# One visit of the array per attention chunk, reads on four quadrants, and two chunks scaled by GpSimd

## The chip, the cores and the metric

One core of a Trainium2 chip runs the whole program. The metric is the device time of one execution in microseconds (us), lower is better. A core has a matmul engine (TensorE, PE in the profile, its weight loads shown apart as PEld), three elementwise engines (VectorE = DVE, ScalarE = ACT, GpSimd = POOL) and a queue that issues transfers (SyncE = SP). Each engine works through its own list of instructions in order; semaphores tie the lists together.

## The reference

```python
# attention: batch 4, 8 heads, 576 positions, head_dim 64
scores = scale * np.matmul(q, k.transpose(0, 1, 3, 2))
gamma = 1.0 - 2.0 ** (-5.0 - np.arange(H))
Dmat = np.where(rel >= 0, gamma[:, None, None] ** rel, 0.0)   # rel = pos_i - pos_j
attn_out = np.matmul(scores * Dmat, v)
x = attn_out.transpose(0, 2, 1, 3).reshape(2304, 512)
# first feed-forward layer, 512 -> 2048 -> 512
h = x @ w_in;  x = np.maximum(0.01 * h, h) @ w_out
# second feed-forward layer, 512 -> 2048 -> 512
h = x @ w_in2; out = (h * np.cos(h)) @ w_out2
```

There is no softmax, so a head's attention can be carried as a running state: what earlier positions give to a query is the query times a 64x64 sum of key-value products.

## The kernel before

**Attention.** The 2304 tokens are cut into 18 chunks of 128, each of two sub-chunks of 64. A chunk's q, k and v for all 8 heads come in one 1 MB transfer (`load_chunk`, into two buffers by turns from chunk 4 on). VectorE scales q (`scale_q`, L219), and ScalarE (chunks 1, 2 and 4 to 7), GpSimd (3) or VectorE (the others) scales v (`scale_v`, L226, L231). Then:

- `scores` (L250): keys times queries, 16 matmuls of 64x64 on all four 64x64 quadrants of the array.
- `masks` (L266): VectorE multiplies the scores by the causal mask into SBUF.
- `values` (L281 and L295): masked scores times v (16 matmuls, L281), and keys times v, which is what the chunk adds to the state (16 matmuls, L295; 8 in a chunk that ends a sequence).
- `states` (L313, L315): VectorE adds that to the running state of each sub-chunk.
- `reads` (L328): state times queries, added to the values in PSUM, 16 matmuls (8 where a sub-chunk begins a sequence). A matmul reads the partitions of one head of a pair and writes the same partitions: only the two quadrants on the diagonal are used.
- `take` (L354): ScalarE scales the result out of PSUM into `xr`.

In the trace every one of these fp32 matmuls has two records, so 16 matmuls read x32.

**First layer.** Tokens go in five blocks (512, 512, 512, 384, 384). For each of 16 slices f of the hidden width there is a group H(j,f) of 12 matmuls (`h_mm`, L451), ScalarE's leaky ReLU out of PSUM (`leaky`, L476 or L741), its split into a high and a low part (L481/L745 on ScalarE, L486/L748 on VectorE), and two steps later a group O(j,f) of 12 matmuls (`o_mm`, L465). In steady state TensorE does H, O, H, O. `h_mm` alternates between two PSUM banks: `hp = psum[:, BANK_H + f % 2, :n]`. PSUM has eight banks: 0 to 3 hold O's sums, 4 and 5 are H's, 6 and 7 are the attention's.

**Order of the work.** Chunks 0 to 3 are done before block 0. Block 0 is written out by hand (the loop over `s` at the end): at step s TensorE does H(0,s), then, where `chunk_at` has a chunk, `values`, the next chunk's `scores` if due, O(0,s-2), `reads`. Meanwhile the weights of this layer are converted from 64-bit words on the fly: per slice VectorE does L397, L399, L403, L410 and, a step later, L422 (the low part), ScalarE L391, L392 and L419. H(0,f) needs L422 of its slice f. Chunks 4 to 7 are used in block 0 and loaded two chunks ahead: after `reads(i)` come `load_chunk(i + 2)` and, for chunks 8 and 9, `scale_q` and `scale_v` on VectorE in the middle of that conversion.

Blocks 1 to 4 and the second layer are ordered by a planner (`Plan`), which is fed tasks with rough durations and due times and plays them; each engine's order comes from it. The second layer is a Strassen-like scheme of `i_mm` (L1062) and an output product (L1191). Its weights are converted during blocks 1 to 4 (L949, L951, L935 to L946).

Of the kernel before, what the change touches and what calls it, by code (L numbers as in the profile page):

```python
# [19 lines left out]
P = 128  # L20
# [35 lines left out]
BANK_O, BANK_H, BANK_A = 0, 4, 6  # L56
# [91 lines left out]
def retention_ffn_ffn(  # L148
# [67 lines left out]
    def scale_q(i):  # L216
        q = ch_t[i][:, 0]

        nc.vector.tensor_tensor(out=q, in0=q, in1=itab_sb, op=ALU.mult)  # L219

    def scale_v(i):
# [8 lines left out]
        eng = nc.gpsimd if 0 < i < n_first else nc.vector  # L230
# [6 lines left out]
    def banks_of(i):  # L237

        return (6, 4, 0, 2)[i] if i < n_first else BANK_A

    def scores(i):
        b, ch = banks_of(i), ch_t[i]
        for p in range(NP):
            for x in range(2):
                for e, r in enumerate(halves):
                    t = slice(p * P + x * C, p * P + (x + 1) * C)
                    nc.tensor.matmul(  # L250
                        psum[halves[x], b + e, p * C : (p + 1) * C],
                        ch[r, 1, t],
                        ch[r, 0, t],
                        start=True,
                        stop=True,
                    )

    def masks(i):
        b = banks_of(i)
# [3 lines left out]
        else:  # L263
            pt = ap.tile([P, 2, NP, C], F32, tag="p", name="p_sb", bufs=1)
        p_t[i] = pt
        nc.vector.tensor_tensor(  # L266
            out=pt,
            in0=psum[:, b : b + 2, : NP * C].rearrange("p e (n c) -> p e n c", n=NP),
            in1=mask_sb.unsqueeze(1).unsqueeze(1).to_broadcast([P, 2, NP, C]),
            op=ALU.mult,  # L270
        )

    def values(i):
        b, ch, pt = banks_of(i), ch_t[i], p_t.pop(i)
        local = [(2 * i + x) % SUBS for x in range(2)]
        for p in range(NP):
            for x, tok in enumerate(halves):
                for e, r in enumerate(halves):
                    h = slice((2 * p + e) * D, (2 * p + e + 1) * D)
                    o = NP * C + p * C  # L280
                    nc.tensor.matmul(  # L281
                        psum[r, b + x, o : o + C],
# [3 lines left out]
                        stop=local[x] == 0,  # L286
                        skip_group_check=True,
                    )
        for p in range(NP):
            for x, tok in enumerate(halves):  # L290
                if local[x] == SUBS - 1:
                    continue
                for e, r in enumerate(halves):
                    h = slice((2 * p + e) * D, (2 * p + e + 1) * D)
                    nc.tensor.matmul(  # L295
                        psum[r, b + x, p * D : (p + 1) * D],
                        ch[tok, 2, h],
                        ch[tok, 3, h],
                        start=False,
                        stop=True,  # L300
                        skip_group_check=True,
                    )

    def states(i):
        b = banks_of(i)
        local = [(2 * i + x) % SUBS for x in range(2)]
        for x in range(2):
            if local[x] == SUBS - 1:
                continue
            new = ap.tile([P, NP * D], F32, tag="st", name="st", bufs=3)  # L310
            add = psum[:, b + x, : NP * D]
            if local[x] == 0:
                summed[i] = nc.vector.tensor_copy(new, add)  # L313
            else:
                summed[i] = nc.vector.tensor_tensor(out=new, in0=add, in1=state[2 * i + x], op=ALU.add)  # L315
            state[2 * i + x + 1] = new

    def reads(i):
        b, ch = banks_of(i), ch_t[i]
        local = [(2 * i + x) % SUBS for x in range(2)]  # L320
        for x in (1, 0):
            if local[x] == 0:
                continue
# [1112 lines left out]
```

## Time and profile before

| | |
|---|---|
| median of 3 runs | 876.35 us (874.76 to 878.08) |
| the profiled execution | 877.37 us, its span 875.6 us |
| PE busy | 847.6 us, 97% of the span |
| DVE busy | 601.1 us, 69% |
| ACT busy | 518.7 us, 59% |
| POOL busy | 1.7 us, 5 instructions |
| DMA | 193.3 MB, 62.7% of 16 engines' time |
| chain that ended last | PE 84%, DMA 7%, DVE 6% |

The span divides into a start (to about 64 us) in which VectorE's conversion sets the pace, blocks 0 to 4 of the first layer (to 495 us), and the second layer. "PEclk" is the clock that TensorE was granted, 1.00 being 2.4 GHz and 0.50 being 1.2 GHz. A row of the timeline is: start, length (us), engine, line, operation, output<-inputs, shapes, count, and in brackets the idle time of the engine before it with what ended it. The lengths of consecutive matmuls overlap slightly, so distances are best taken from start to start.

### The profile page before, as it was taken

Reading aid. Unit: us, or ns where it says so; the run is one execution under the profiler, and the core shown is the slowest. Engines: PE = TensorE matmul, PEld = TensorE weight load, DVE = VectorE, ACT = ScalarE, POOL = GpSimd, SP = SyncE. Lnnn points to the kernel's source line nnn. Section 1 sums busy time; section 2 is a strip of 40 time slices with the busy share of each in tenths; the row PEclk is TensorE's granted clock in tenths of the full one; section 3 lists DMA queues with packets and bytes.
Section 4 is the critical chain, followed back from the end, with each engine's and each line's share of the span. In section 5 each row is a group of like instructions: output and inputs, shape, how many; then the busy total and the mean of one; then the engine's idle time right before and its main releaser. Section 6 shows DMA issues by size and latency. Waiting matters only on the chain.

```text
span 875.6 us, 16272 instructions
## 1 busy us (share of the span) xinstructions
PE 847.6 (97%) x6288; PEld 779.3 (89%) x6288; DVE 601.1 (69%) x1187; ACT 518.7 (59%) x1112; POOL 1.7 (0%) x5
## 2 busy tenths in 40 slices
PE   6699979999999999999999999999999999999998
PEld 6577767778887888899999989999999999999998
DVE  5799684767776676676631278888897876765772
ACT  4787753545455545555632388777678765777650
POOL 0000000000000000000000000000000000000000
PEclk8899989999999999999999999999999999999999
DMA  9925402557657666665476398979988798474311
GB/s 360 417 78 208 158 1 86 173 177 230 188 215 232 182 230 192 230 207 191 147 293 270 88 315 283 335 249 409 310 288 264 260 369 334 158 268 181 132 49 73
DMA packets 91949, 193.30 MB, mean 221 GB/s; under 512 B 7648, under 2 KB 55264, under 8 KB 81632
## 3 DMA queue, kind: packets, MB, share of 16 engines
q1 hardware_dynamic: 91728, 191.92, 62.7%
q8 instruction: 49, 0.80, 0.4%
q10 hardware_dynamic: 144, 0.35, 0.1%
q14 instruction: 28, 0.23, 0.1%
HBM read 143.22 MB, written 49.02 MB: 220 GB/s over the span
## 4 chain that ended last, share of the span: by engine, by line
PE 84%; DMA 7%; DVE 6%; issue 1%; ACT 1%; SPq 0%; DVEq 0%; ACTq 0%
PE psum L1191 22%; PE psum L465 19%; PE psum L451 19%; PE psum L1062 19%; DMA ch<-in_qkv 4%; PE psum L328 2%; PE psum L250 1%; PE psum L281 1%; DMA mraw<-in_w 1%; PE psum L295 1%; DMA xq<-m 1%; DVE w L422 1%; DVE t L410 1%; DVE t L403 1%; DMA ws<-ws 1%
## 5 line engine op out<-in xcount | busy, mean ns | idle before, releaser
L451 PE MATMUL psum<-x_sb,w 128*128 128x512 f32 (+1 forms) x960 | 218.4, 377 | 10.6 <-DVE w L422 7.2
L1191 PE MATMUL psum<-g,wo 128*128 128x384 f32 x1152 | 222.3, 334 | 0.0
L465 PE MATMUL psum<-g,w 128*128 128x512 f32 (+1 forms) x960 | 214.4, 373 | 0.0
L451 PEld LDWEIGHTS psum<-x_sb,w 128*128 128x128 f32 x960 | 177.3, 191 | 37.5 <-DVE w L422 8.3
L1191 PEld LDWEIGHTS psum<-g,wo 128*128 128x128 f32 x1152 | 201.7, 188 | 0.0
L465 PEld LDWEIGHTS psum<-g,w 128*128 128x128 f32 x960 | 173.8, 188 | 24.4 <-DVE graw L704 0.4
L1062 PE MATMUL psum<-x,ws 128*128 128x384 f32 x576 | 114.5, 335 | 1.8 <-ACT psum L1164 1.3
L1062 PEld LDWEIGHTS psum<-x,ws 128*128 128x128 f32 x576 | 100.9, 188 | 2.8 <-ACT psum L1164 1.9
L748 DVE TENSOR_TENSOR g<-graw,g 128x512 fp32r<-128x512 f32 (+1 forms) x64 | 39.9, 624 | 68.4 <-ACT g L745 67.7
L1062 PE MATMUL psum<-x,wa 128*128 128x384 f32 x432 | 86.1, 334 | 0.0
L1062 PEld LDWEIGHTS psum<-x,wa 128*128 128x128 f32 x432 | 75.9, 188 | 0.0
L745 ACT CAST g<-graw 128x512 fp32r<-128x512 f32 (+1 forms) x64 | 36.2, 566 | 63.0 <-PE psum L465 62.5
L1118 DVE SCALAR_TENSOR_TENSOR h<-r,h 128x384 f32<-128x384 f32 x96 | 52.9, 553 | 24.5 <-ACT r L1115 24.2
L741 ACT ACTIVATE graw<-psum 128x512 f32<-128x512 f32 (+1 forms) x64 | 34.8, 543 | 51.4 <-PE psum L451 49.3
L1114 ACT ACTIVATE r<-r 128x384 f32<-128x384 f32 x96 | 50.4, 525 | 21.4 <-DVE r L1107 20.9
L1102 DVE SCALAR_TENSOR_TENSOR r<-n,h 128x384 f32<-128x384 int32 x96 | 52.9, 551 | 11.9 <-ACT n L1099 11.6
L1128 DVE TENSOR_TENSOR g<-h,g 128x384 fp32r<-128x384 f32 x96 | 52.6, 552 | 11.1 <-ACT g L1125 10.4
L1099 ACT ACTIVATE n<-h 128x384 int32<-128x384 f32 x96 | 49.3, 518 | 8.4 <-DVE h L1091 8.0
L1107 DVE SCALAR_TENSOR_TENSOR r<-n,r 128x384 f32<-128x384 int32 x96 | 53.1, 553 | 1.6
L1125 ACT CAST g<-h 128x384 fp32r<-128x384 f32 x96 | 48.6, 509 | 7.2 <-DVE h L1118 6.9
L1115 ACT ACTIVATE r<-r 128x384 f32<-128x384 f32 x96 | 50.5, 526 | 2.0
L1210 DVE SCALAR_TENSOR_TENSOR acc<-psum,acc 128x384 f32<-128x384 f32 x48 | 26.7, 556 | 16.4 <-PE psum L1191 15.3
(80 smaller groups left out, 795.8 us busy)
## 6 DMA issues: line engine op xcount, KB each, us to landing
ws<-ws SPq DMA_DIRECT2D x24, 1024.0 KB, 7.0
wo<-wo SPq DMA_DIRECT2D x24, 1024.0 KB, 6.5
wa<-wa SPq DMA_DIRECT2D x24, 768.0 KB, 6.4
ch<-in_qkv SPq DMA_DIRECT2D x17, 1024.0 KB, 7.4
mraw<-in_w SPq DMA_DIRECT2D x64, 256.0 KB, 3.4
x<-xq SPq DMA_DIRECT2D x21, 768.0 KB, 9.6
raw<-in_w SPq DMA_DIRECT2D x15, 1024.0 KB, 10.4
xq<-m SPq DMA_DIRECT2D x84, 128.0 KB, 5.0
```

Source lines behind the costliest of these rows:

```text
L451: nc.tensor.matmul(hp, wt[:, i, cols], x_t[lj, k][:, j, :n], start=(k == 0 and a == 0), stop=(k == KK - 1 and a == 2),)
L465: nc.tensor.matmul(psum[:, BANK_O + m, :n], wt[:, i, cols], gt[:, j, :n], start=(f == 0 and a == 0), stop=(f == NF - 1 and a == 2),)
L1062: nc.tensor.matmul(bank[BANKS[m]], a[:, hl, i, j * P : (j + 1) * P], x[:, j, v, :], start=m in (1, 5) and j == 0 and n == 0, stop=j == 1 a ...
L1099: t = add("ACT", 515, lambda: nc.scalar.activation(n_ap(), hb.ap, AF.Copy, scale=INV_2PI), [t], due, 0, nb.old)
L1102: nc.vector.scalar_tensor_tensor(out=r_ap(), in0=n_ap(), scalar=-C1, in1=hb.ap, op0=ALU.mult, op1=ALU.add)
L1107: nc.vector.scalar_tensor_tensor(out=r_ap(), in0=n_ap(), scalar=-C2, in1=r_ap(), op0=ALU.mult, op1=ALU.add)
L1114: t = add("ACT", 515, lambda: nc.scalar.activation(r_ap(), r_ap(), AF.Sin, scale=0.5), [t], due)
L1115: t = add("ACT", 515, lambda: nc.scalar.activation(r_ap(), r_ap(), AF.Square), [t], due)
L1118: nc.vector.scalar_tensor_tensor(out=hb.ap, in0=r_ap(), scalar=0.5, in1=hb.ap, op0=ALU.subtract, op1=ALU.mult)
L1125: t = add("ACT", 515, lambda: nc.scalar.copy(gb.ap[:, 0], hb.ap), [t], due, 0, gb.old)
L1128: nc.vector.tensor_tensor(out=gb.ap[:, 1], in0=hb.ap, in1=gb.ap[:, 0].bitcast(F32), op=ALU.subtract)
L1191: nc.tensor.matmul(bank[m], wt[:, i, hl, m * P : (m + 1) * P], gt[:, v, :], start=h == 0 and z == 0 and x == 0, stop=h == 1 and z == 1 and ...
```

## The change

1. **One visit.** `values(i)`, the first half of `reads(i)`, the state products of the next chunk (split off from `values` as `growth(i + 1)`), `scores(i + 1)` and the second half of `reads(i)` now follow one another directly, as `visit(i)`. `masks(i + 1)`, `states(i + 1)` and `take(i)` come after it. A `visit(3)` at step 3 of block 0 holds only `growth(4)` and `scores(4)`. So chunk i + 1 must be scaled (q and v) before visit(i).
2. **Four quadrants.** The values of odd head pairs are written to the other half of the partitions, and `reads` is split into two parts by sub-chunk and head, so that four consecutive matmuls lie in four quadrants. The host turns the matching halves of the first layer's weight rows and of a scale table.
3. **Waits through GpSimd.** Between parts that write one PSUM bank from different row halves, GpSimd executes an empty instruction that waits for TensorE, and TensorE waits for GpSimd (`rows_done`).
4. **Banks.** The attention takes banks 5, 6 and 7. H uses bank 4 for every f, but bank 5 for f = 1, so H(j,f) must wait for the leaky ReLU of H(j,f-1), from f = 3 on.
5. **Scaling.** q and v of chunks 8 and 9 are scaled by GpSimd. Chunks 5 to 7 are scaled up to two steps earlier than before.

```diff
-        nc.vector.tensor_tensor(out=q, in0=q, in1=itab_sb, op=ALU.mult)
+        eng = nc.gpsimd if n_busy <= i < n_busy + 2 else nc.vector
+        eng.tensor_tensor(out=q, in0=q, in1=itab_sb, op=ALU.mult)
...
-        eng = nc.gpsimd if 0 < i < n_first else nc.vector
+        eng = nc.gpsimd if 0 < i < n_busy + 2 else nc.vector
...
+        b = BANK_A
+        return [(b, 0), (b + 1, 0)], [(b + 1, NP * C), (b + 2, NP * C)], [(b, NP * C), (b + 2, 0)]
...
+    def rows_done(behind):
+        got = nc.gpsimd.engine_nop()
+        in_turn(got, behind)
+        return got
...
                     h = slice((2 * p + e) * D, (2 * p + e + 1) * D)
-                    o = NP * C + p * C
-                    nc.tensor.matmul(
-                        psum[r, b + x, o : o + C],
+                    b, o = v[x]
+                    got = nc.tensor.matmul(
+                        psum[halves[e ^ p % 2], b, o + p * C : o + (p + 1) * C],
                         ch[tok, 3, h],
                         pt[tok, e, p, :],
...
+    def reads(i, part):
+        v, ch = banks_of(i)[1], ch_t[i]
+        behind = [last_of.pop("rows")] if part else []
+        for p in range(NP):
+            for e, r in enumerate(halves):
+                x = e ^ part
+                if tokens_of(i)[x] == 0:
+                    continue
+                b, o = v[x]
+                t = p * P + x * C
+                last_of["pe", i] = nc.tensor.matmul(
+                    psum[halves[e ^ p % 2], b, o + p * C : o + (p + 1) * C],
+                    state[2 * i + x][r, p * D : (p + 1) * D],
+                    ch[r, 0, t : t + C],
...
+    def visit(i):
+        if i >= n_first:
+            values(i)
+            reads(i, 0)
+        if i + 1 < NCH:
+            growth(i + 1)
+            scores(i + 1)
+        if i >= n_first:
+            reads(i, 1)
...
-        hp = psum[:, BANK_H + f % 2, :n]
+        hp = psum[:, BANK_H + (f == 1), :n]
...
+        visits = {t: i for t, i in chunk_at.items() if i < n_busy}
+        visits[FIRST_CHUNK - 1] = n_first - 1
         for s in range(NF):
-            i = chunk_at.get(s)
+            i = visits.get(s)
             h_mm(0, s)
             if i is not None:
-                values(i)
-            if s + 1 in chunk_at:
-                scores(chunk_at[s + 1])
+                visit(i)
             leaky(0, s)
...
-            if n_first <= chunk_at.get(s + 2, 0) < n_busy:
-                scale_q(chunk_at[s + 2])
-                scale_v(chunk_at[s + 2])
+            if s + 1 in visits and visits[s + 1] + 1 < n_busy:
+                scale_q(visits[s + 1] + 1)
+                scale_v(visits[s + 1] + 1)
```

TensorE around chunk 6 in block 0, before. L250 is scores of chunk 6, L281 and L295 its values and state products, L328 its reads; L451 are H groups and L465 O groups, w_... the slice's weights:

```order
L250 MATMUL psum<-ch 64x64 x16
L465 MATMUL psum<-g,w_790 128x512 x12
L451 MATMUL psum<-x_sb,w_996 128x512 x12
L281 MATMUL psum<-p_sb,ch 64x64 x16
L295 MATMUL psum<-ch 64x64 x16
L465 MATMUL psum<-g,w_856 128x512 x12
L328 MATMUL psum<-ch,st 64x64 x16
L451 MATMUL psum<-x_sb,w_1062 128x512 x12
```

The same engine now, around chunk 5. L305 is its values, L366 its reads in two parts, L328 and L268 the state products and scores of chunk 6; L505 are H, L519 O:

```order
L505 MATMUL psum<-x_sb,w_843 128x512 x12
L305 MATMUL psum<-p_sb,ch 64x64 x16
L366 MATMUL psum<-ch,st 64x64 x8
L328 MATMUL psum<-ch 64x64 x16
L268 MATMUL psum<-ch 64x64 x16
L366 MATMUL psum<-ch,st 64x64 x8
L519 MATMUL psum<-g,w_670 128x512 x12
```

Three interruptions of the H and O groups per chunk have become one.

TensorE at step 3 of block 0, before, with the engines that each instruction waits for. w_568 is slice 3, so the first row is the end of H(0,3); L250 is scores of chunk 4, w_514 O(0,1):

```order
L451 MATMUL psum<-x_sb,w_568 128x512 x10
L250 MATMUL psum<-ch 64x64 [waits DMAHW2_49,DVE_49]
L250 MATMUL psum<-ch 64x64 x15
L465 MATMUL psum<-g,w_514 128x512
L465 MATMUL psum<-g,w_514 128x512 [waits Activation_49]
```

The same place now (w_572 is slice 3, L328 the state products of chunk 4, L268 its scores, w_518 O(0,1)):

```order
L505 MATMUL psum<-x_sb,w_572 128x512 x10
L328 MATMUL psum<-ch 64x64 [waits DMAHW2_49,Activation_49]
L328 MATMUL psum<-ch 64x64 [waits Activation_49] x7
L268 MATMUL psum<-ch 64x64 [waits DVE_49]
L268 MATMUL psum<-ch 64x64 x15
L519 MATMUL psum<-g,w_518 128x512 x12
```

Ahead of the scores now stand the state products, each of which waits for ScalarE's scaling of one head of v.

VectorE in block 0 where chunk 8 is scaled, before. L219 and L231 scale chunk 8, L410 ends the conversion of slice 12's words (t_1059) and L422 makes its low part (w_1135); L397 and L399 are slice 13's, L315 is states, L486 the low part of a hidden group:

```order
L410 ISA t_1059<-raw,t_1059 128x2048
L315 TENSOR_TENSOR st<-psum,st 128x256 x2
L486 TENSOR_TENSOR g<-graw,g 128x512
L219 TENSOR_TENSOR ch<-ch,tabs_sb 128x512
L231 TENSOR_TENSOR ch<-ch,tabs_sb 128x512
L397 TENSOR_SCALAR t_1132<-t_1132 128x1024
L399 TENSOR_SCALAR t_1132<-t_1132 128x1024
L422 TENSOR_TENSOR w_1135<-t_1059,w_1135 128x1024
```

And now (t_1089 and w_1206 are slice 12, L288 is masks, L351 states):

```order
L464 ISA t_1089<-raw,t_1089 128x2048
L288 TENSOR_TENSOR p_sb<-psum,tabs_sb 128x512
L351 TENSOR_TENSOR st<-psum,st 128x256 x2
L540 TENSOR_TENSOR g<-graw,g 128x512
L451 TENSOR_SCALAR t_1203<-t_1203 128x1024
L453 TENSOR_SCALAR t_1203<-t_1203 128x1024
L476 TENSOR_TENSOR w_1206<-t_1089,w_1206 128x1024
```

The two scalings are gone from VectorE's list there, and with them their wait for chunk 8's transfer.

## Rows read from the trace of the kernel before

**Rows 1.** Waits of PE, 64 to 500 us: who for whom, total, times, longest.
```profile
PE psum L451 <- DVE w L422: 6.4, 2, 4.4
PE psum L328 <- DVE st L315: 0.6, 1, 0.6
```

**Rows 2.** Timeline of PE over one chunk in block 1.
```profile
204.75 0.69 PE L250 MATMUL psum<-ch 64*64 64x64 f32 x32
205.37 3.02 PE L465 MATMUL psum<-g,w 128*128 128x512 f32 x12
...
211.04 0.69 PE L281 MATMUL psum<-p_sb,ch 64*64 64x64 f32 x32
211.56 0.65 PE L295 MATMUL psum<-ch 64*64 64x64 f32 x32
212.13 3.02 PE L465 MATMUL psum<-g,w 128*128 128x512 f32 x12
215.08 1.15 PE L328 MATMUL psum<-ch,st 64*64 64x64 f32 x32
216.16 3.02 PE L451 MATMUL psum<-x_sb,w 128*128 128x512 f32 x12
219.02 2.88 PE L465 MATMUL psum<-g,w 128*128 128x512 f32 x12
221.74 2.88 PE L451 MATMUL psum<-x_sb,w 128*128 128x512 f32 x12
```

**Rows 3.** Timeline of DVE in block 0, a conversion and a wait.
```profile
96.66 1.22 DVE L422 TENSOR_TENSOR w<-t,w 128x1024 fp32r<-128x1024 f32 x1
...
110.27 0.69 DVE L219 TENSOR_TENSOR ch<-ch,tabs_sb 128x512 f32<-128x512 f32 x1 [8.54 <-DMA ch<-in_qkv]
```

**Rows 4.** Timeline of PE at the same places.
```profile
103.70 3.02 PE L451 MATMUL psum<-x_sb,w 128*128 128x512 f32 x12
...
114.08 1.22 PE L451 MATMUL psum<-x_sb,w 128*128 128x512 f32 x2 [4.42 <-DVE w L422]
...
119.08 0.89 PE L250 MATMUL psum<-ch 64*64 64x64 f32 x32
...
138.70 3.98 PE L451 MATMUL psum<-x_sb,w 128*128 128x512 f32 x11 [2.01 <-DVE w L422]
142.48 8.81 PE L465 MATMUL psum<-g,w 128*128 128x512 f32 x36
```

**Rows 5.** Windows, block 0: length, PE, PEld, DVE, ACT, POOL busy, PEclk, DMA.
```profile
114.00:120.00 6.00, 5.92 (x44) 4.33 (x44) 5.93 (x8) 5.80 (x13) 0.00 (x0) 0.54 0.00 0
```

**Rows 6.** Timeline at steps 3 and 4 of block 0, PE and ACT.
```profile
52.74 3.05 PE L465 MATMUL psum<-g,w 128*128 128x512 f32 x12
52.97 2.02 ACT L226 ACTIVATE ch<-ch,tabs_sb 128x64 f32<-128x64 f32 x8
...
63.36 0.68 PE L328 MATMUL psum<-ch,st 64*64 64x64 f32 x16 [0.74 <-DVE st L313]
```

**Rows 7.** Timeline of PE and ACT at the start of block 3.
```profile
358.81 2.27 PE L451 MATMUL psum<-x_sb,w 128*128 128x384 f32 x12
359.36 0.49 ACT L741 ACTIVATE graw<-psum 128x384 f32<-128x384 f32 x1 [0.96 <-DMA y<-graw]
```

**Rows 8.** Waits of the whole span, one of ScalarE's.
```profile
ACT mraw L949 <- DMA mraw<-in_w: 19.2, 16, 2.5
```

**Rows 9.** Timeline of PE and POOL in the start.
```profile
7.60 0.69 PE L250 MATMUL psum<-ch 64*64 64x64 f32 x32
9.11 0.69 PE L281 MATMUL psum<-p_sb,ch 64*64 64x64 f32 x32 [0.81 <-DVE p_sb L266]
...
19.02 1.48 POOL L231 TENSOR_TENSOR ch<-ch,tabs_sb 128x512 f32<-128x512 f32 x1 [18.57 <-DMA ch<-in_qkv]
...
28.50 0.80 PE L328 MATMUL psum<-ch,st 64*64 64x64 f32 x20 [2.59 <-issue]
```

**Rows 10.** Groups by line, VectorE's masks.
```profile
L266 DVE TENSOR_TENSOR p_sb<-psum,tabs_sb 128x512 f32<-128x512 f32 x18 | 12.4, 687 | 4.8 <-PE psum L250 4.6
```

More of the change, by code (lines that the diff above doesn't have):

```diff
@@ L314, in states @@
             else:
-                summed[i] = nc.vector.tensor_tensor(out=new, in0=add, in1=state[2 * i + x], op=ALU.add)
+                got = nc.vector.tensor_tensor(out=new, in0=add, in1=state[2 * i + x], op=ALU.add)
             state[2 * i + x + 1] = new
[L318 to L323, printed above, removed]
-            st = state.pop(2 * i + x)
-            for p in range(NP):
-                for r in halves:
-                    o, t = NP * C + p * C, p * P + x * C
-                    read = nc.tensor.matmul(
-                        psum[r, b + x, o : o + C],
-                        st[r, p * D : (p + 1) * D],
-                        ch[r, 0, t : t + C],
-                        start=False,
-                        stop=True,
-                        skip_group_check=True,
-                    )
-                    if i in summed:
-                        tc.add_manual_dep(
-                            read.ins, summed.pop(i).ins.name, IN_TURN, reason="other rows"
-                        )
@@ L343, in take @@
-    def take(i):
-        b = banks_of(i)
+            last_of["st", i] = got
+    def reads(i, part):
[12 more added lines that the diff above has]
+                    ch[r, 0, t : t + C],
+                    start=False,
+                    stop=True,
+                    skip_group_check=True,
+                )
+                while behind:
+                    in_turn(last_of["pe", i], behind.pop())
+                if ("st", i) in last_of and i < n_first:
+                    in_turn(last_of["pe", i], last_of.pop(("st", i)))
+        if not part:
+            last_of["part", i] = last_of["rows"] = rows_done(last_of["pe", i])
@@ L359, in take @@
                 )
+                if i >= n_first and i + 1 < NCH and p == 0 and x0 == 0:
+                    in_turn(got, last_of["st", i + 1])
+                last_of["take", i] = got
     def warm(n, bank):
@@ L598, in rest @@
                 if i is not None:
-                    new.append(("values", i))
-                if s + 1 in chunk_at:
-                    new.append(("scores", chunk_at[s + 1]))
+                    new.append(("visit", i))
             o = steps[s - LAG]
@@ L636, in rest @@
         slots += todo
-        LONG = {"scores": 0.9, "values": 1.5, "reads": 0.6}
         def ffn_long(j):
@@ L1261, in rest @@
         flows.sort()
-        do = {"H": ffn_h, "O": ffn_o, "i": unit, "o": out_,
-              "scores": attention, "values": attention, "reads": attention}
+        do = {"H": ffn_h, "O": ffn_o, "i": unit, "o": out_, "visit": attention}
         for slot in slots:
@@ L1375, in retention_ffn_ffn @@
                 o_mm(0, s - LAG)
-            if i is not None:
-                reads(i)
+            if i is not None and i >= n_first:
                 take(i)
```

161 lines of the change are left out of this document (97 added, 64 removed).

## The prediction

> **What bounds the kernel now.** I read the waits first, then the timelines of PE and VectorE, then the clock. Between 64 and 500 us TensorE waits for nothing but two things: 6.4 us in two waits for VectorE's low part of the weights (L422), and 0.6 us for one state [rows 1]. Apart from these, time in the first layer is what TensorE's instructions take, so a shorter list of attention work is worth its full length there. The reader should see in [rows 2] what a chunk costs. From start to start, scores take 0.62 us (204.75 to 205.37), values 0.52, state products 0.57 and reads 1.08 (215.08 to 216.16): 2.79 us. An undisturbed group of 12 takes 2.72 (219.02 to 221.74); the group behind an interruption takes 2.86 (216.16 to 219.02), and one that has an interruption on both sides 2.95 (212.13 to 215.08). So going into small matmuls costs 0.09 and coming out 0.14 us, 0.23 for each of three interruptions, 0.69. A whole chunk costs 3.48 us.
>
> The two long waits come from one step further back. VectorE stands still for 8.54 us at L219, which scales chunk 8 and waits for its transfer [rows 3]; TensorE runs out of weights, waits 4.42 us [rows 4], and its clock falls to 1.2 GHz for most of the next 6 us (granted 0.54) [rows 5]. Chunk 9 repeats it with 2.01 us. Until then VectorE is ahead: L422 of slice 11 ends at 97.88 [rows 3], H(0,11) starts at 103.70 [rows 4], 5.8 us later.
>
> **The change part by part.**
>
> *Interruptions.* Chunks 4 to 17 lose two of three: 14 x 2 x 0.23 = 6.44 us. The instructions themselves stay, and the groups of H and O are the same.
>
> *Reads.* 16 matmuls (32 records) on two quadrants take 1.08 us; values, the same shape on four, take 0.52, state products 0.57 [rows 2]. I take 0.54, so half a chunk's reads go from 0.54 to 0.27. Of 28 half-chunks in chunks 4 to 17 three begin a sequence and have no reads: 25 x 0.27 = 6.75 us. In the start (chunks 0 to 3) reads are followed by other waits; I count nothing, with 0.5 us either way.
>
> *States in time.* States of a chunk are now made three steps before they are read. The waits of 0.74 us at 63.36 [rows 6] and 0.6 us [rows 1] go: 1.34 us.
>
> *Chunks 8 and 9 on GpSimd.* VectorE's list has no wait for a transfer in it any more. Gone are TensorE's waits of 4.42 and 2.01 us. Behind the first H(0,12) took 5.00 us (114.08 to 119.08) instead of 2.72, a loss of 2.28; behind the second 11 matmuls took 3.78 us (138.70 to 142.48) instead of 11/12 of 2.72, a loss of 1.29 [rows 4]. Together 10.0 us. What is late next would be VectorE's conversion itself. It was 5.8 us ahead. TensorE now needs about 2 us less for the two visits before slice 12, the visit at step 3 (below) gives it 4 us more, and VectorE does the same work less four scalings. GpSimd takes 1.48 us for one such scaling [rows 9]; it has a chunk's distance (some 19 us) for the transfer and two of them. So I count no new wait.
>
> How far the two share a port is not shown by the one row of GpSimd. The Trainium skill, SBUF — State Buffer, section Who interferes with whom, says that a VectorE instruction with two SBUF inputs and a GpSimd instruction that reads SBUF exclude each other, the second one waiting for the first to end. By that rule VectorE could lose up to 2 x 1.48 = 2.96 us per chunk, which the lead covers; only rival C below would lose by it.
>
> *The visit at step 3.* This part costs. Chunk 4's state products now stand ahead of its scores, and each waits for one head of v from ScalarE. ScalarE scales v from 52.97 to 54.99; TensorE went on with O(0,1) at 52.74 [rows 6]. Now it can't before the last head's product and the scores: 54.99 + 0.1 + 0.62 = 55.7. That is 2.96 us later, less 0.3 for the products that are done there and not later: 2.7 us. The gap in front of it is over 2 us of full idleness and then a trickle. After idle times of 2.01 and 4.42 us the clock was at half speed for a while, with losses of 1.29 and 2.28 us [rows 4, 5]. I take 1.3, bounds 0 and 2.3. ScalarE and VectorE are not delayed by it: they have the same list up to there.
>
> *One bank for H.* H(j,f) now waits for the leaky ReLU of f - 1 instead of f - 2; O(j,f-2) lies in between, 2.72 us or, in blocks 3 and 4, about 2.1. ScalarE's leaky ReLU takes 0.5 to 0.6. At the start of block 3 one ended at 359.36 + 0.49 = 359.85, held up by a store, and the next H began at 358.81 [rows 7]: it would wait 1.04. I take 1.5 in all. Bounds: 0, since the planner's order is new, and 6, if ScalarE's longest wait for a transfer, 2.5 us [rows 8], stood ahead of a leaky ReLU some three times with 2 us showing each time.
>
> *Waits through GpSimd.* The trace shows no empty instruction there. TensorE's scores to values with VectorE in between took 1.51 us (7.60 to 9.11) [rows 9], of which 0.62 are the scores and 0.69 the mask [rows 10]; 0.2 remain for two crossings. The empty instruction should need less than a mask, so a round trip is between 0.2 and 0.9 us. In a visit the first has the state products beside it (0.57), the second the scores (0.62). I take 0.3, nearer to the crossing alone, so nothing shows; the upper end would cost 0.3 twice per visit, 14 x 0.6 = 8.4 us.
>
> *The sum*, against the profiled execution's own 877.37 us: -6.44 - 6.75 - 1.34 - 10.0 + 2.7 + 1.3 + 1.5 = -19.0, that is 858.3. The median of the runs lies 1.0 us under that execution: 857.3 us. The second layer has the same order as before on TensorE, and I take it as unchanged.
>
> **The rivals.**
>
> A. The forecast: 857.3, between 852 (no clock loss, no bank wait, a little gained in the start) and 863 (the worse ends of both).
>
> B. The round trips through GpSimd show, up to 8.4 us: 865.7. For it: two such waits in each visit, and visits whose state products are halved leave only 0.3 us of cover. Against: the 0.2 us that two crossings take.
>
> C. VectorE is not far enough ahead in block 0, because the clock, the late masks of chunk 5 and GpSimd's share of its port add up. One wait of about 3 us with a clock loss of 2.3 remains: 862.6; two of them 868. For it: TensorE ran dry there before. Against: the lead of 5.8 us.
>
> D. Reads don't run four at a time: the 6.75 us stay, 864.1. For it: parts of one bank are written from different halves of the rows, and no row shows this pattern. Against: values show four quadrants with the same shapes.
>
> E. Slower than before: TensorE's instructions run dry. A visit is 128 records in a row with as many weight loads, where the longest run in the steady state has 64. In the start, after some 200 records in a row, TensorE stood for 2.59 us and waited for nothing that the profile shows ("issue"), which fits a fetch of instructions that came late [rows 9]. If each of 14 visits had that, it would be 14 x 2.59 = 36 us: 893. From 1.36 us per visit on the change is a loss. Against: after 64 us TensorE has no such wait at all [rows 1].
>
> **How the numbers follow.** A 0.64, B 0.10, C 0.14, D 0.06, E 0.06. A measurement of this kernel can tell about 0.5%, 4.4 us, from no change: under 872 is faster. A is all there. B, C and D are mostly there too; of each I put a part beyond its price to no change (0.03, 0.02, 0.01), and of E 0.01, with 0.05 for slower. So faster 0.88, no change 0.07, slower 0.05. The range reaches from 851 to 867: all of A, most of B, C and D.
>
> **What would show each step.** In a chunk of block 1, about 18.8 us from visit to visit in place of 19.8, with a visit near 2.3 us from its first small matmul to the next group, and no gap of PE before L268's second record or the second part of L366. In block 0, no wait of VectorE at L220 and no wait of PE for L476 near slices 12 and 15; PE idle some 3 to 4 us before L328 at step 3 with ScalarE's L227 as releaser, and PEclk under 1.00 behind it. Waits of L505 for L790 at the starts of blocks would be the bank; 1 to 2 us in all. The forecast is wrong if the visits take 3 us or more, or if PE's list shows "issue" or GpSimd as a releaser inside them.

## The result, and the profile after

The changed kernel takes 853.58 us (median of four runs, 853.00 to 855.49) against 875.74 (874.76 to 878.08): a ratio of 0.9747, interval 0.9721 to 0.9772. The forecast was 857.3, with a range of 851 to 867, and faster. Run again later, on the chip of the last three experiments, the same kernel took 855.77 (854.81 to 855.95) against 875.64, ratio 0.9774 (0.9756 to 0.9791). So the medians differ by 22.2 us the first time and by 19.9 the second. The profiled execution is one of 853.42 us with a span of 851.3, so 23.95 us less than the one of before. Its stretch up to the second layer went from 494.91 to 471.05 us, 23.9 less, and only 0.4 us of the span's 24.3 lie behind that. First row of the second layer on TensorE, before and after:

```profile
494.91 1.20 PE L1062 MATMUL psum<-x,wa 128*128 128x384 f32 x6
```
```profile
471.05 1.20 PE L1111 MATMUL psum<-x,wa 128*128 128x384 f32 x6
```

TensorE's waits between 64 and 500 us, against [rows 1] (for whom, total, times, longest):

```profile
PE psum L1111 <- ACT psum L1212: 1.3, 1, 1.3
PE psum L366 <- POOLq L255: 0.2, 1, 0.2
```

The first is at 481 us, in the second layer. Both waits for VectorE's low part of the weights and the wait for a state are gone. What the change put in as a wait (an empty instruction of GpSimd, L255) shows once in this stretch, 0.2 us in the last chunk, where no state products lie between the two halves of the reads.

One chunk in block 1, the counterpart of [rows 2]. Timeline of TensorE; L305 is values, L366 the reads in two parts, L328 and L268 the next chunk's state products and scores, L505 and L519 are H and O:

```profile
194.21 2.88 PE L505 MATMUL psum<-x_sb,w 128*128 128x512 f32 x12
197.02 0.69 PE L305 MATMUL psum<-p_sb,ch 64*64 64x64 f32 x32
197.54 0.41 PE L366 MATMUL psum<-ch,st 64*64 64x64 f32 x16
197.77 0.65 PE L328 MATMUL psum<-ch 64*64 64x64 f32 x32
198.24 0.65 PE L268 MATMUL psum<-ch 64*64 64x64 f32 x32
198.70 0.41 PE L366 MATMUL psum<-ch,st 64*64 64x64 f32 x16
199.05 1.66 PE L519 MATMUL psum<-g,w 128*128 128x512 f32 x6
```

Read it from start to start. The visit takes 2.03 us (197.02 to 199.05); 2.3 was forecast. In its middle 32 records take 0.47 us (197.77 to 198.24 to 198.70), at its first edge 0.52. A whole period, from values to values, is 18.57 us (197.02 to 215.59), where it was 19.80 (211.04 in [rows 2] to 230.84). So a chunk became 1.23 us shorter; 1.0 was forecast (0.46 of interruptions, 0.54 of reads). Counted in the two timelines, TensorE leaves its large groups for small matmuls 42 times between 50 us and the second layer before, and 15 times now: once for each of the chunks 4 to 17, and once at step 3. So 27 interruptions are gone.

VectorE and GpSimd where chunk 8 is scaled, against [rows 3] (timelines):

```profile
101.56 1.23 DVE L464 CUSTOM_DVE_ANT_0 t<-raw,t 128x2048 uint16<-128x2048 uint16 x1
...
106.03 1.22 DVE L476 TENSOR_TENSOR w<-t,w 128x1024 fp32r<-128x1024 f32 x1
...
108.42 2.21 DVE L464 CUSTOM_DVE_ANT_0 t<-raw,t 128x2048 uint16<-128x2048 uint16 x1
110.55 1.53 DVE L540 TENSOR_TENSOR g<-graw,g 128x512 fp32r<-128x512 f32 x1
```
```profile
107.44 2.10 POOL L220 TENSOR_TENSOR ch<-ch,tabs_sb 128x512 f32<-128x512 f32 x1 [86.86 <-DVE w L476]
109.49 2.03 POOL L232 TENSOR_TENSOR ch<-ch,tabs_sb 128x512 f32<-128x512 f32 x1
```

VectorE no longer waits for a transfer there. But the two engines hold each other up: L464 takes 2.21 us in place of 1.23 and L540 1.53 in place of 0.68 (its length at 104.10) while GpSimd is at work, so VectorE loses 1.8 us. GpSimd's two take 2.10 and 2.03. For chunk 9 in the second profile of this kernel (last experiment), with VectorE standing or held up itself, they take 1.29 and 1.04:

```profile
127.03 1.29 POOL L220 TENSOR_TENSOR ch<-ch,tabs_sb 128x512 f32<-128x512 f32 x1 [14.88 <-DMA ch<-in_qkv]
128.28 1.04 POOL L232 TENSOR_TENSOR ch<-ch,tabs_sb 128x512 f32<-128x512 f32 x1
```

Of this the Trainium skill, SBUF — State Buffer, section Who interferes with whom, has the rule: a VectorE instruction with two SBUF inputs and a GpSimd instruction that reads SBUF shut each other out. The trace agrees (2.21 for 1.23, 1.53 for 0.68), and VectorE's lead covered the loss.

The windows of block 0 and of the start (length, PE, PEld, DVE, ACT, POOL busy, PEclk, DMA), against [rows 5]:

```profile
11.00:21.50 10.50, 6.86 (x216) 6.33 (x218) 8.39 (x12) 7.51 (x24) 1.48 (x1) 0.51 1.01 417
28.00:38.50 10.50, 6.25 (x61) 4.74 (x62) 6.36 (x10) 7.23 (x15) 0.00 (x0) 0.51 1.02 420
45.00:49.00 4.00, 4.00 (x12) 3.12 (x11) 3.93 (x6) 3.24 (x5) 0.00 (x0) 0.57 0.47 187
64.00:142.00 78.00, 77.97 (x736) 64.21 (x727) 65.82 (x85) 54.32 (x98) 6.83 (x4) 1.00 0.39 133
```

From 64 to 142 us TensorE is busy throughout at the full clock (granted 1.00): the two falls of block 0 are gone. The start, though, has three falls to half speed, at 11 to 21, 28 to 38 and 45 to 49 us. The profile of before has two there (14 to 24 and 34 to 38).

Step 3, against [rows 6] (timeline of TensorE, and ScalarE's L227):

```profile
51.46 2.97 PE L505 MATMUL psum<-x_sb,w 128*128 128x512 f32 x12
54.37 2.02 ACT L227 ACTIVATE ch<-ch,tabs_sb 128x64 f32<-128x64 f32 x8
54.77 1.94 PE L328 MATMUL psum<-ch 64*64 64x64 f32 x15 [0.34 <-ACT ch L227]
...
57.16 3.06 PE L519 MATMUL psum<-g,w 128*128 128x512 f32 x12
...
62.91 0.69 PE L305 MATMUL psum<-p_sb,ch 64*64 64x64 f32 x32
```

As forecast, the state products of chunk 4 trickle behind ScalarE (1.94 us). But TensorE stands idle before them for 0.34 us and not for 3 to 4, since it came to them 2.95 us later than before and ScalarE only 1.40. O(0,1) starts at 57.16, 4.42 us later than in [rows 6], and chunk 4's values at 62.91 in place of 58.48.

### The profile page after: what moved, and what is told of

Read it like the earlier page. It is cut to its first block, busy times and chain, and to the rows that moved or that the text cites. A ratio compares the mean times of both kernels' runs of the same rounds, so it can differ in the third digit from the quotient of the medians.

```text
span 851.3 us, 16302 instructions
## 1 busy us (share of the span) xinstructions
PE 829.3 (97%) x6288; PEld 771.0 (91%) x6288; DVE 601.5 (71%) x1183; ACT 518.4 (61%) x1112; POOL 8.5 (1%) x9
## 4 chain that ended last, share of the span: by engine, by line
PE 90%; DMA 4%; issue 3%; DVE 2%; ACT 1%; SPq 0%; POOLq 0%; DVEq 0%
PE psum L1239 23%; PE psum L519 22%; PE psum L505 21%; PE psum L1111 19%; DMA raw<-in_w 2%; PE psum L366 1%; PE psum L305 1%; PE psum L328 1%; PE psum L268 1%; DMA wa<-wa 1%; DMA ws<-ws 1%; DVE t L464 0%; DVE st L351 0%; DVE t L457 0%; DVE t L453 0%
## 5 line engine op out<-in xcount | busy, mean ns | idle before, releaser
L505 PE MATMUL psum<-x_sb,w 128*128 128x512 f32 (+1 forms) x960 | 214.2, 373 | 4.2 <-DVE x_sb L493 2.5
L519 PE MATMUL psum<-g,w 128*128 128x512 f32 (+1 forms) x960 | 212.0, 370 | 0.0
L505 PEld LDWEIGHTS psum<-x_sb,w 128*128 128x128 f32 x960 | 177.5, 190 | 29.7 <-DVE x_sb L493 2.7
L519 PEld LDWEIGHTS psum<-g,w 128*128 128x128 f32 x960 | 174.3, 188 | 23.7
L1150 DVE SCALAR_TENSOR_TENSOR r<-n,h 128x384 f32<-128x384 int32 x96 | 53.0, 552 | 11.9 <-ACT n L1147 11.5
L1176 DVE TENSOR_TENSOR g<-h,g 128x384 fp32r<-128x384 f32 x96 | 52.7, 553 | 10.9 <-ACT g L1173 10.3
```

The source lines that it names most:

```text
L505: nc.tensor.matmul(hp, wt[:, i, cols], x_t[lj, k][:, j, :n], start=(k == 0 and a == 0), stop=(k == KK - 1 and a == 2),)
L519: nc.tensor.matmul(psum[:, BANK_O + m, :n], wt[:, i, cols], gt[:, j, :n], start=(f == 0 and a == 0), stop=(f == NF - 1 and a == 2),)
L1150: nc.vector.scalar_tensor_tensor(out=r_ap(), in0=n_ap(), scalar=-C1, in1=hb.ap, op0=ALU.mult, op1=ALU.add)
L1176: nc.vector.tensor_tensor(out=gb.ap[:, 1], in0=hb.ap, in1=gb.ap[:, 0].bitcast(F32), op=ALU.subtract)
```

## The experiments

All go against the kernel before on the same chip. A stretch that no fall of the clock touches is compared in the timelines too, since the start alone moves the time of one kernel by some us (last experiment). "More" and "less" for a variant of the changed kernel are counted from 853.58 us where nothing else is said. The same kernel took 855.77 on the chip of the last three, so by the total alone some 2 us can't be told.

**Ninth and tenth chunk on VectorE again.**

```diff
-        eng = nc.gpsimd if n_busy <= i < n_busy + 2 else nc.vector
-        eng.tensor_tensor(out=q, in0=q, in1=itab_sb, op=ALU.mult)
+        nc.vector.tensor_tensor(out=q, in0=q, in1=itab_sb, op=ALU.mult)
...
-        eng = nc.gpsimd if 0 < i < n_busy + 2 else nc.vector
+        eng = nc.gpsimd if 0 < i < n_first else nc.vector
```

> The changed kernel, with the ninth and tenth chunk scaled by VectorE again; all else as changed. Theory (the prediction's term of 10.0 us): VectorE stands still at L219's successor for the transfers of chunks 8 and 9, TensorE runs out of converted weights near slices 12 and 15 with a fall of its clock behind each: 853.6 + 8 to 10, that is 861.5 to 863.6, with waits of TensorE for the low part of the weights of about 4 and 2 us. Rival 1: the later start of block 0 and the 1.5 us that step 3 lost give VectorE a lead that covers most of it: 853.6 + 0 to 4. Rival 2: since a chunk's q and v are now needed one step earlier, the stand costs more than before: over 865.

857.05 us (854.43 to 858.06), ratio 0.9782 (0.9758 to 0.9807): 3.5 more, rival 1. VectorE and TensorE of this run:

```profile
101.24 1.22 DVE L475 TENSOR_TENSOR w<-t,w 128x1024 fp32r<-128x1024 f32 x1
...
109.30 0.69 DVE L219 TENSOR_TENSOR ch<-ch,tabs_sb 128x512 f32<-128x512 f32 x1 [2.45 <-DMA ch<-in_qkv]
...
111.84 1.22 DVE L475 TENSOR_TENSOR w<-t,w 128x1024 fp32r<-128x1024 f32 x1
```
```profile
112.62 3.29 PE L504 MATMUL psum<-x_sb,w 128*128 128x512 f32 x12
116.11 3.03 PE L518 MATMUL psum<-g,w 128*128 128x512 f32 x12 [0.21 <-DVE g L539]
```

VectorE stands for 2.45 us in place of 8.54 [rows 3]. H(0,12) is stretched by 0.4 us, with 0.2 of a wait behind it, where it waited 4.42 [rows 4]. Count from the start of chunk 6's values (102.29, before 98.58): slice 12's low part is ready after 10.8 us (111.84 + 1.22), before after 15.5 (112.81 + 1.22). The buffer that chunk 8 goes into comes free with chunk 6's reads, and those now lie in the visit. So its load is issued 2.2 us behind that start (104.45), before it was 5.3 (103.86): 3.1 of the 4.7 us. The other 1.6 are the transfer, from issue to VectorE's start 4.9 us in place of 6.4; why it was shorter no run shows. The time is rival 1's, but its reason (a lead by the later start) is not what the rows show: the load follows TensorE's reads, and a later start moves both. So the visit cures by itself most of what GpSimd was to cure.

**GpSimd's scaling alone**, in the kernel before:

```diff
-        nc.vector.tensor_tensor(out=q, in0=q, in1=itab_sb, op=ALU.mult)
+        eng = nc.gpsimd if n_busy <= i < n_busy + 2 else nc.vector
+        eng.tensor_tensor(out=q, in0=q, in1=itab_sb, op=ALU.mult)
...
-        eng = nc.gpsimd if 0 < i < n_first else nc.vector
+        eng = nc.gpsimd if 0 < i < n_busy + 2 else nc.vector
```

> The kernel before, with only the ninth and tenth chunk scaled by GpSimd. Theory (the prediction's term): the two waits of TensorE (4.42 and 2.01 us) and the losses of clock behind them (2.28 and 1.29) go and nothing is late in their place: 875.7 - 10.0 = 865.7. Rival 1: behind the removed waits TensorE meets VectorE's conversion itself a few slices on, 2 to 5 us stay: 868 to 871. Rival 2: GpSimd, at 1.5 to 2.1 us for a scaling, holds VectorE up as well: over 871.

867.44 us (867.12 to 867.90), ratio 0.9910 (0.9889 to 0.9930), 8.2 less than the kernel before there (875.61). No wait for the low part of weights is left. The start of this run lost 1.9 us against the profile of before (chunk 4's values at 60.41 in place of 58.48). Behind it the term is there in full, and larger than forecast, as the table of the next experiment shows: 11.1 us. Chunk 4's values and the start of the second layer in this run, for a sum further below:

```profile
60.41 0.69 PE L282 MATMUL psum<-p_sb,ch 64*64 64x64 f32 x32
...
485.72 1.20 PE L1063 MATMUL psum<-x,wa 128*128 128x384 f32 x6
```

**VectorE keeps the scaling, two steps later in its list**, in the kernel before:

```diff
                 if i + 2 >= n_busy:
-                    scale_q(i + 2)
-                    scale_v(i + 2)
+                    late[min(s + 2, NF - 1)] = i + 2
+            if s in late:
+                scale_q(late[s])
+                scale_v(late[s])
```

> The kernel before, with VectorE's scalings of chunks 8 and 9 two steps further back in its list; GpSimd takes no part. Theory: what cost time was the place in VectorE's list (a wait for a transfer, ahead of the weights of slices 12 and 15), not VectorE's 0.69 us for each scaling; so this cures nearly as much as GpSimd did: between chunk 6's values and the second layer 9 to 11 us less than the kernel before (GpSimd alone: 11.1), about 867. Rival: VectorE's own work is what is late, and GpSimd helped by taking 2.7 us of it away: 2 to 4 us less, about 872.

866.91 us (866.28 to 867.54), ratio 0.9903 (0.9887 to 0.9919): the same as with GpSimd. So it was the place in the list, a wait ahead of the weights, and not VectorE's work. From the start of chunk 6's values to that of the second layer, in the timelines of TensorE:

| | scaled in the old place | GpSimd | two steps later |
|---|---|---|---|
| old order of attention | 396.33 | 385.22 (-11.1) | 385.39 (-10.9) |
| one visit | 373.40 (-22.9) | 370.87 (-25.5) | |

The two parts bring 34.0 us one by one and 25.5 together: 8.6 us are the same waits, removed twice. Behind the visits GpSimd is worth 2.5 us.

**Reads on two quadrants**, in the changed kernel (twice, values and reads; the host's turns undone):

```diff
-                        psum[halves[e ^ p % 2], b, o + p * C : o + (p + 1) * C],
+                        psum[r, b, o + p * C : o + (p + 1) * C],
```

> The changed kernel with its odd head pairs not turned, so that reads run on two quadrants (the diagonal ones); one visit, GpSimd's waits and scaling as changed. By the sizes that the trace of the changed kernel shows (eight reads in a half, 16 records, about 0.23 us on four quadrants and 0.47 on two): 25 x 0.235 = 5.9 us more, 859.4, and a visit of 2.02 + 0.47 = 2.49 us. By the prediction's size (0.27 a half): 6.75 more, 860.3. Rival: reads are limited by something other than quadrants (the rate at which records are issued, one state half at a time): 853.6 to 855.

862.88 us (859.25 to 863.30), ratio 0.9849 (0.9821 to 0.9877); the profiled execution took 860.11, 6.7 more than the changed kernel's. That median is more than either size gives; the timelines tell the reads apart from the start. The 14 periods are 0.40 to 0.48 us longer each (chunk 6 to 7: 19.04 for 18.57), and from chunk 4's values to the second layer they sum to 6.4 us (414.52 for 408.14), 0.46 a chunk. So reads on two quadrants do take twice the time. But this is not yet what the change gained by four quadrants. All 14 chunks lose here, and chunks 4, 9 and 13 had nothing to lose against the old order. In them one sub-chunk begins a sequence; the eight reads of the other are now made in two parts of four, and the four of a part lie on two quadrants (on one in this experiment). From chunk 9's values to chunk 10's, before 191.71 to 211.04, after 178.51 to 197.02:

```profile
191.71 0.69 PE L281 MATMUL psum<-p_sb,ch 64*64 64x64 f32 x32
```
```profile
178.51 0.69 PE L305 MATMUL psum<-p_sb,ch 64*64 64x64 f32 x32
```

That period became 0.82 us shorter (19.33 to 18.51) and chunk 13's 0.83, where a whole chunk's became 1.23: two interruptions, and nothing for reads. A whole chunk's reads gain 0.47 (19.04 to 18.57), so four quadrants gained 11 x 0.47 = 5.2 us, where 6.75 was forecast.

**The visit cut in two**, with a quarter of H between:

```diff
-            h_mm(0, s)
+            h_mm(0, s, range(KK - 1))
+            if i is not None:
+                visit_a(i)
+            h_mm(0, s, (KK - 1,))
             if i is not None:
                 visit(i)
...
```

(`visit_a` is values and the first half of the reads; the planner's blocks likewise.)

> The changed kernel with its visit cut in two: values and the first half of the reads stand ahead of the last quarter (three matmuls) of H, the rest of the visit behind it. The same small matmuls, 14 interruptions more. By the size that the trace of the changed kernel suggests (0.38 us an interruption, both ends of the small matmuls included): 14 x 0.38 = 5.3 more, 858.9. By the prediction's size (0.23): 3.2 more, 856.8. Rival: the weight loads of small matmuls hide behind H and an interruption costs nothing by itself: 853.6 to 854.5.

860.33 us (859.18 to 860.59), ratio 0.9826 (0.9802 to 0.9849), 6.8 more, of which 5.6 lie between chunk 4's values and the second layer. TensorE at the chunk of the rows above (L507 is H, L521 O):

```profile
200.94 0.69 PE L305 MATMUL psum<-p_sb,ch 64*64 64x64 f32 x32
201.46 0.41 PE L366 MATMUL psum<-ch,st 64*64 64x64 f32 x16
201.80 0.97 PE L507 MATMUL psum<-x_sb,w 128*128 128x512 f32 x3
202.70 0.69 PE L328 MATMUL psum<-ch 64*64 64x64 f32 x32
203.21 0.65 PE L268 MATMUL psum<-ch 64*64 64x64 f32 x32
203.68 0.41 PE L366 MATMUL psum<-ch,st 64*64 64x64 f32 x16
204.02 2.35 PE L521 MATMUL psum<-g,w 128*128 128x512 f32 x9
```

The three matmuls of H take 0.90 us where a quarter of 2.72 is 0.68: 0.22 at the large matmuls' side, as the prediction had it. The small ones take 0.86 + 1.32 = 2.18 in place of 2.03: 0.15 more on their own side. The period is 18.96 for 18.57. An interruption costs 0.39 us. With the reads' 0.47 this gives the period: 2 x 0.39 + 0.47 = 1.25, where a chunk became 1.23 shorter. The Trainium skill, TensorEngine Tiling (Array Packing), section Key Properties, states that a change of the tiling mode drains TensorE. The 0.39 us agree with it in so far as each change costs; no run here tells a drain from another cost at the seam.

**One bank for H**, in the kernel before:

```diff
-        hp = psum[:, BANK_H + f % 2, :n]
+        hp = psum[:, BANK_H + (f == 1), :n]
```

> The kernel before, with H in one bank from its third slice on, as in the change; all else as before. Theory (the trace of the changed kernel, which has no wait of H for a leaky ReLU): O(j,f-2) always covers it, 875.7 within 1 us. By the prediction's term: 1.5 more, 877.2, with waits of H for L790's counterpart at the starts of blocks. Rival: three long waits of ScalarE show with 2 us each: 881.

876.93 us (875.22 to 878.16), ratio 1.0014 (1.0005 to 1.0024): 1.2 more. At block 3's start, the place of [rows 7], TensorE now has

```profile
359.21 2.38 PE L451 MATMUL psum<-x_sb,w 128*128 128x384 f32 x12 [0.89 <-ACT graw L741]
```

where 1.04 was read off beforehand, and no other such wait. So in the old order the wait that the prediction read off is there (0.89 us, of a term of 1.5); the theory of the expectation (always covered) falls. In the changed kernel the same leaky ReLU, again held up by a store, ends in time:

```profile
338.40 0.49 ACT L790 ACTIVATE graw<-psum 128x384 f32<-128x384 f32 x1 [0.52 <-DMA y<-graw]
```
```profile
337.54 2.26 PE L519 MATMUL psum<-g,w 128*128 128x384 f32 x12
339.64 2.28 PE L505 MATMUL psum<-x_sb,w 128*128 128x384 f32 x12
```

O covers it with 0.75 us to spare (338.89 to 339.64). Three variants of the changed kernel did have one wait of H for a leaky ReLU, 0.4 to 0.7 us, all in block 2.

**Chunks 4 to 7 on GpSimd too.**

```diff
-        eng = nc.gpsimd if n_busy <= i < n_busy + 2 else nc.vector
+        eng = nc.gpsimd if n_first <= i < n_busy + 2 else nc.vector
...
-        if i in (1, 2) or n_first <= i < n_busy:
+        if i in (1, 2):
```

> The changed kernel, with chunks 4 to 7 scaled by GpSimd too (q and v of each), so six chunks in place of two. Theory: at step 3 chunk 4's v is there long before its state products, so the 0.34 us of idle and the slow trickle of 1.94 us (0.46 would do) in front of the scores go: 853.6 - 1.8 = 851.8. Rival 1: VectorE, which shares its time in the scratch memory with GpSimd, gets late with the weights in slices 4 to 10: 2 to 6 us slower. Rival 2: the step's delay reappears as a wait for the weights of slice 4, since VectorE and not chunk 4 sets the time there: 853.6.

855.01 us (854.17 to 856.27), ratio 0.9766 (0.9749 to 0.9784): no gain that the runs can tell. The trickle at step 3 is gone, but in the start GpSimd's scaling falls on VectorE's split of x (four L493; the last row is the changed kernel's):

```profile
34.09 1.38 POOL L220 TENSOR_TENSOR ch<-ch,tabs_sb 128x512 f32<-128x512 f32 x1 [0.33 <-DMA ch<-in_qkv]
35.42 1.50 POOL L232 TENSOR_TENSOR ch<-ch,tabs_sb 128x512 f32<-128x512 f32 x1
```
```profile
33.64 4.43 DVE L493 TENSOR_TENSOR x_sb<-xr,x_sb 128x512 fp32r<-128x512 f32 x4 [2.00 <-ACT x_sb L492]
```
```profile
34.09 2.50 DVE L493 TENSOR_TENSOR x_sb<-xr,x_sb 128x512 fp32r<-128x512 f32 x4 [2.24 <-ACT x_sb L492]
```

They take 4.43 us in place of 2.50, every weight behind them comes later (TensorE waits 2.13 us for slice 2's at 44.29, 0.89 in the changed kernel), and chunk 4's values start at 63.50 in place of 62.91. It is rival 1, with the start and not slices 4 to 10 as its place.

**More work for TensorE in the start**, 20 matmuls on zeros:

```diff
         growth(0)
+        warm(12, 3)
...
         both_reads(3)
+        warm(8, 7)
```

> The changed kernel with 20 more matmuls on zeros in the start, in two places where TensorE waits: 12 behind chunk 0's state products, 8 behind chunk 3's reads. Theory: the 2.95 us that block 0's fourth slice starts later than before are the clock alone (half speed from 28.1 to 38.4 us and from 45.2 to 48.6), and an engine that is kept busy keeps its clock: H(0,3) starts 1 to 3 us earlier, 850.6 to 852.6. Rival 1: the clock falls in spite of it, because the stand of 2.19 us in which TensorE waits for nothing that the profile shows is what sets it off: 853.6, and the fall is seen behind that stand again. Rival 2: more instructions make that stand longer: 854 to 856.

855.90 us (854.64 to 857.44), ratio 0.9776 (0.9757 to 0.9795): no gain. The clock fell all the same, from 20 to 37 us; the eight matmuls ran at half speed, 3.78 us, and H(0,0) began at 35.83 in place of 34.84. H(0,3) began at 51.02, 0.4 earlier, and behind the wait for chunk 4's v (1.92 us here) the clock fell again: values at 65.47. The theory falls. What the zeros did move is the first fall: it came at 20 us here and at 22 in the next run, and between 10 and 15 us in the eleven profiles without them. H(0,0) was not earlier for it. With both edits:

> Both together: six chunks scaled by GpSimd and 20 more matmuls on zeros in the start. Theory: the two gains add up, 853.6 - 1.8 - 1 to 3 = 848.8 to 850.8. Rival: an earlier TensorE in block 0 only waits for VectorE's conversion, which has no more lead there: 851 to 853.6.

856.36 us (856.26 to 858.87), ratio 0.9787 (0.9769 to 0.9806). Chunk 4's values start at 62.72; nothing adds up.

**Chunk 4's v one place earlier in ScalarE's list.**

```diff
             ready(s + 3)
+            if s == FIRST_CHUNK - 2:
+                scale_v(n_first)
             high_of(s + 2)
...
-                scale_v(visits[s + 1] + 1)
+                if visits[s + 1] >= n_first:
+                    scale_v(visits[s + 1] + 1)
```

> The changed kernel, with ScalarE's scaling of chunk 4's v (eight heads, 2.02 us) one place earlier in its list, ahead of the cast of slice 4's weights; all else as changed. Theory: at step 3 every head is there when H(0,3) ends, so the idle time and the trickle of state products (1.94 us in place of 0.46) go, 1.8 us as in the profile of the changed kernel, and up to 4.4 where the wait is 1.9 us and TensorE's clock falls behind it (as in three of the variants): the same chip's time of the changed kernel less 1.8 to 4.4. Slice 4's weights come 1.2 us later, over 4 us before they are needed. Rival 1: the cast of slice 4's weights is on the path after all, as with GpSimd's scaling of chunk 4 (where slice 2's came 1.2 us later): 0 to +1. Rival 2: what TensorE gains there it gives back in a later wait for VectorE's conversion, since VectorE has no lead at step 3: 0.

852.72 us (852.52 to 853.74), ratio 0.9744 (0.9726 to 0.9761), against 855.77 for the changed kernel on this chip: 3.0 less, and no run of the one reaches one of the other. It is the fastest version of these, by little. ScalarE at step 3 and at chunk 5, and TensorE at the same places:

```profile
52.09 2.01 ACT L227 ACTIVATE ch<-ch,tabs_sb 128x64 f32<-128x64 f32 x8
...
79.51 2.02 ACT L227 ACTIVATE ch<-ch,tabs_sb 128x64 f32<-128x64 f32 x8
```
```profile
51.57 2.95 PE L505 MATMUL psum<-x_sb,w 128*128 128x512 f32 x12
54.45 0.51 PE L328 MATMUL psum<-ch 64*64 64x64 f32 x10
...
55.53 3.05 PE L519 MATMUL psum<-g,w 128*128 128x512 f32 x12
...
61.23 0.69 PE L305 MATMUL psum<-p_sb,ch 64*64 64x64 f32 x32
...
80.73 1.13 PE L328 MATMUL psum<-ch 64*64 64x64 f32 x29
```

H(0,3) starts 0.1 us off the first profile of the changed kernel, and chunk 4's values 1.7 earlier (61.23): the theory's 1.8. Part goes back at once: chunk 6's state products take 1.13 us (80.73), since ScalarE's v is now the late one there (79.51 + 2.02 = 81.53), and at the second layer 0.9 are left. Against the changed kernel's profile on the same chip (next experiment) it is 2.4 us at chunk 4's values and 1.5 at the second layer. In all those two profiles differ by 2.3, and the 0.8 behind the start of the second layer is not explained.

**The changed kernel once more**, unchanged:

> The changed kernel once more, on the same chip as the two others. Theory: TensorE's clock falls in the start at other times from one execution to the next, and this alone moves block 0's slice 3 (51.46 us in the first profile) by 1 us and chunk 4's values (62.91) by up to 2.5 us, with the same list on every engine; 853 to 857. Rival: the start of the changed kernel is the same in every execution: 51.4 to 51.5 and 62.9.

H(0,3) starts at 52.14 and chunk 4's values at 63.59, 0.7 later than in the first profile. Other runs with the same order of instructions in the start have 50.51 and 65.03 (VectorE's scaling), 51.39 and 62.79 (two quadrants), 50.92 and 64.52 (visit cut in two). A first half-speed spell begins between 10 and 15 us in all of them. The later ones lie elsewhere each time: 28 to 38 and 45 to 49 us in the first profile, 22.5 to 39.5 and 46 to 50 in this one, 30 to 40.5 and 57 to 61 with VectorE's scaling:

```profile
57.00:61.00 4.00, 4.00 (x43) 3.29 (x42) 3.97 (x7) 3.49 (x4) 0.00 (x0) 0.57 0.02 4
```

There the wait at step 3 is 1.9 us and the spell follows it, as in the run with the visit cut in two. Where the spell came just ahead, TensorE arrived later and waited 0.33 to 0.36. The old list moves too: chunk 4's values at 58.48, 60.41, 60.69 and 60.06 us in four profiles, 59.9 in the mean, against 63.8 for the five of the changed list.

## Why the prediction was right, point by point

The way, the range and the parts of the list that save time were right. The sum came out 3.7 us too slow by the medians (857.3 for 853.58), and its terms were less right than that.

| term | forecast | shown | by |
|---|---|---|---|
| interruptions | -6.44 (28 x 0.23) | -10.5 (27 x 0.39) | the cut visit, the count |
| reads | -6.75 (25 halves) | -5.2 (11 chunks x 0.47) | two quadrants, periods |
| states in time | -1.34 | -1.3, the waits are gone | waits after |
| chunks 8 and 9 | -10.0 | -11.1 | GpSimd alone (later place: -10.9) |
| step 3, its clock, the start | +4.0 | +3.9 in the two profiles | timelines |
| one bank | +1.5 | 0; 0.9 in the old order | rows of block 3 |
| GpSimd's round trips | 0 | +0.2 | waits after |

Step 3 and start: 62.91 - 58.48 = 4.4, less 0.5 for chunk 4's state products, which now come ahead (16 records on two quadrants, the time of 32 on four: 0.47). The shown terms make -24.0 us; up to the second layer the profiled executions differ by 23.9. One comparison does without the start and without the waits for weights: from chunk 4's values to the second layer GpSimd alone took 425.3 us (60.41 to 485.72) and the changed kernel 408.1 (62.91 to 471.05). These are 17.2 less. Interruptions, reads, two waits for states (1.4 in that run), the 0.5 and the 0.2 make 17.4.

- **The mis-sized term is the interruption.** The prediction read its 0.23 us off the large groups beside it (0.09 going in, 0.14 coming out). The small matmuls have an edge too: 32 records take 0.47 us inside a run, but 0.62, or 1.09 for 64, between two large groups [rows 2], and this 0.15 to 0.16 was booked as work. It also counted 28 where 27 fell away, as the visit at step 3 is an interruption of its own. 10.5 in place of 6.4 is 4.1 of the 5.0 us between the sum of -19.0 and -24.0. The bank's 1.5 and 1.1 of chunks 8 and 9 lie on the same side, 1.6 of the reads on the other; that one error took back part of the others is luck.
- **Reads.** The mechanism holds: two quadrants take twice the time of four, 0.47 us a chunk, 0.235 a half where 0.27 was taken. The count doesn't: in the three chunks in which a sequence begins, the other half gains nothing, so 22 halves and not 25. Rival D is out.
- **Chunks 8 and 9.** The term was 1.1 us short. A part of it is in the first loss of clock: 5.00 us for H(0,12) were set against 12 matmuls, but one of them had run ahead of the wait, at 109.28, and the scores behind took 0.82 us in place of 0.62. The sum took the waits once, and rightly. What it said of the cause was too narrow: it credited GpSimd, but the visits alone remove 8.6 of the 11.1 us and a later place on VectorE 10.9. Rival C, VectorE not far enough ahead, did not occur; 1.8 us lost to GpSimd were covered.
- **Step 3 and the start.** The mechanism (state products behind ScalarE) holds. That the sum (4.0) agrees is in part luck, since the division doesn't hold: in the first profile 2.95 us came before step 3, where the prediction had 0 with 0.5 either way, and 1.5 at it, with no fall of the clock behind. From H(0,3)'s start to chunk 4's values the five profiles of this list took 11.4 to 11.5 us three times, and 14.5 and 13.6 where the wait was 1.9 us and the clock did fall behind it; the four of the old list took 9.2 to 10.0. So step 3 costs about 1.5 us or about 4, depending on how far TensorE is ahead of ScalarE there. With zeros, too, the wait was 1.9 us and the clock fell (O(0,1) took 4.0 us; 4.2 with VectorE's scaling). What sets the times of the falls is open: more work for TensorE moved them and did not stop them.
- **Bank and GpSimd's round trips.** Zero and 0.2, within the bounds given. 0.3 us was the value taken for a round trip; the last chunk shows 0.2 of idle. Rival B is out.
- **Rival E** (instructions run dry): between 64 and 500 us no wait of TensorE's matmuls is put down to "issue". It is out.

## What to carry to other kernels

Price a change of matmul shape from both sides of the seam, by comparing a run of small matmuls inside a longer one with the same run between large ones; the neighbours alone showed 0.22 of 0.39 us here. Count the seams and the gains in the instruction list and not by chunk: the cases at the edges of a sequence gained nothing here. When two parts of a change touch the same late resource, don't add them up: ask which wait each removes, for the second removal brings nothing. Before moving work to another engine to get a wait out of an in-order list, try moving it down the list.

## What the chip showed that I had not expected

- TensorE's switch between 128 x 128 and 64 x 64 matmuls and back costs 0.39 us in all, 0.22 on the large side and 0.15 on the small; on four quadrants 64 records take 0.93 us in the middle of a run (197.77 to 198.70), 14.5 ns each (one matmul has two records).
- GpSimd's two 128 x 512 multiplications take 1.29 and 1.04 us with VectorE standing or held up, and 2.10 and 2.03 beside a working VectorE, which itself lost 1.8 us to them; at 34 us it lost 1.9.
- A wait of TensorE for GpSimd's empty instruction, itself behind TensorE, showed 0.2 us bare and nothing behind 0.47 us of other matmuls.
- Half-speed spells in the start of one and the same list lay elsewhere in each execution and moved chunk 4's values by 2.2 us (62.8 to 65.0).
